# A fused attention and two-FFN kernel: the first token pair goes over to seven-product form two hidden blocks earlier, and the steps in front of it are laid out anew

## The chip, the cores and the metric

The kernel runs on one core of one Trainium2 chip. The metric is the device time of one execution in microseconds (us); the kernel before takes 1032.87 us (median of 3 runs, 1032.5 to 1033.78). The engines are called PE (TensorE), DVE (VectorE), ACT (ScalarE), POOL (GpSimd) and SP (SyncE, which issues loads).

## The reference

Everything is fp32. Tokens N = 6016, width C = 256, hidden width 2048.

```python
qn = q / (norm(q, axis=1) + 1e-6);  kn = k / (norm(k, axis=1) + 1e-6)
a  = softmax(kn.T @ qn / tau)                    # 256 x 256
x  = v @ a                                       # 6016 x 256
h  = x @ w_in;   x1 = (h * sigmoid(1.702 * h)) @ w_out
h2 = x1 @ w2_in; out = (max(h2, 0) + alpha * min(h2, 0)) @ w2_out
```

q, k, v and x arrive as fp32. The weights reach the device as 8-byte words (`raw`), which the kernel turns into fp32 with bit and multiply steps.

## The kernel before, in words

**Products in three passes.** Each fp32 operand is split into a high and a low part in fp32r; a product is three matmuls of 128 x 512 (`PASSES`: high x high, weight-high x token-low, weight-low x token-high), summed in PSUM (`product`, line 783).

**Tiling.** Tokens come in 12 chunks, two by two: a pair p holds chunks 2p and 2p+1. The hidden width is 16 tiles, taken two by two: j = 0..7. For one pair and one j, the first matrix (`WI`) gives four hidden blocks ("units"), each through an activation on ACT (`act`), a cast to its high part on ACT (`high`) and a subtraction on DVE (`low`, line 878). The second matrix (`WO`) then adds each unit into output accumulators in PSUM. Those 24 matmuls (`Outs.next`, called eight times) are laid between the products of the next j.

**Two ways to the four units.** `direct` (line 884) takes eight products. `quartet` (line 906) takes seven, in Strassen's manner, in the order A11, S1, A12, S2, S3, A22, S4. It needs sums of weight blocks (S1 to S4, made by `combine`: one whole-sum step, four small sums, a cast on ACT, a low word on DVE) and sums of token blocks (T1 to T4, made by `prepare`, each again with a subtraction, an ACT cast and a DVE low word). S2's result is copied out of its bank by ACT before S3's product adds to the same bank (`copy(a)`). In the first pair of layer 1 (l = 0), j < `STRASSEN` = 6 runs `direct`, the last two j run `quartet`; all later pairs run `quartet`.

**The first pair makes its own weights.** Attention is folded into the first matrix: W = E^T W1I is computed on PE while the first pair runs. For j >= 4 this goes by pairs of j (`emit_pair`, line 717): two halves m of six matmuls (`pw`), each kept by ACT (`activation`, the high part) and DVE (`scalar_tensor_tensor`, the low part). A "place" is one unit of `direct`: place 4j+i. `PAIRS` gives the place of pair 4 (j = 4, 5) as 13 and of pair 6 (j = 6, 7) as 21. The tiles that hold the converted W1I (`wi_hi`, `wi_lo`, line 339) have one buffer each: what is converted for pair 6 goes where pair 4's lay.

**Conversion.** A W1I or W1O piece goes through `scale` (ACT), `shift`, `power`, `rest` (DVE), `copy` (the high part, ACT), and then either `less` and `low` (two DVE steps) or, for pieces with `added`, a summing DMA from POOL (`sent`) and one DVE step (`split`). Three raw buffers hold loads; a load is asked for when an earlier piece's `rest` is done.

**What sets the order.** The program order on each engine is written by `beside(time)` (line 750): after each unit it pours DVE steps into a budget of microseconds, taking the step with the earliest `due` from the conversion and from the list `bg`. ACT's casts are put off into a list and emitted at the next `beside`. `need` and `finish` force what must be done. Each engine's instructions stand in the order in which they are written.

Of the kernel before, what the change touches and what calls it, by code (L numbers as in the profile page):

```python
# [30 lines left out]
FREE = ((0.7, 2.8, 1.7), (0.0, 0.8, 0.8))  # L31
FIRST = 2.1
AHEAD = 2
QK_PARTS = [1, 3] + [4] * 9 + [2, 2, 2, 1]
TAIL = 12
LOADING = 3
LANDING = 3
STRASSEN = 6
ON_VECTOR = (4, 5, 6, 8)
# [7 lines left out]
def f32(ap):  # L47
    return ap.bitcast(F32)
# [11 lines left out]
def attention_then_two_ffns(ctx: ExitStack, tc: tile.TileContext, q, k, vT, tau, w1i, w1o, w2i, w2o, alpha, outT):  # L60
# [129 lines left out]
    class Converter:  # L190


        STEPS = (("shift", 0.45), ("power", 0.45), ("rest", 0.63), ("less", 0.63), ("low", 0.63))
        ADDED = (("shift", 0.45), ("power", 0.45), ("rest", 0.63))

# [30 lines left out]
        def time(self, piece):  # L226
            if not piece or self.landed():
                return 0.63
            return self.list(piece)[self.at][1]
# [35 lines left out]
        def step(self):  # L265

            if self.waits():
                if not self.open:
                    self.scale(True)
                scalar_work()  # L270
            if not self.next() or self.landed():
                self.settle()
                return 0.63
# [35 lines left out]
        def due(self):  # L309
            return min(x.due for x in self.left())  # L310

        def place(self):
            self.now += 1
            if self.ahead and Convert.deep:
                self.scale()
                if self.flying and self.now - self.flying[0].begun >= LANDING:
                    self.ask()
# [13 lines left out]
    with tc.manual_schedule():  # L331
# [26 lines left out]
        def outer(j, n=1):  # L358
            def pair():
                return tuple(WO[:, j:j + n, h].rearrange("p q a b -> p q (a b)") if n > 1 else flat(WO[:, j, h]) for h in range(2))  # L360
            return Convert(w1o[:, j * PIECE:(j + n) * PIECE].rearrange("p (a n) -> p a n", a=1), pair, added=j > 3)

# [267 lines left out]
        def prepare(l, p):  # L630
# [20 lines left out]
            def minus(nm, a, b):  # L651
# [4 lines left out]
                ("B11", B11), ("B21", B21), ("T1", None), ("T2", None), ("T3", None), ("T4", None), ("B22", B22))}  # L656
            D = 0.63
            early = [
# [18 lines left out]
            if (l, p) == (0, 0):  # L677
                def last():
                    ops["T4"] = operand()
                    tmp["T4"] = tmp["T2"]  # L680
                    minus("T4", B21, "T2")
                steps = [early[i] for i in (2, 3, 6, 7)] + [late[0], Step(D, None, last, hi["T4"])] + [late[i] for i in (4, 5)]
                for x, due in zip(steps, (4, 4, 4, 4, 3, 3, 3, 3)):
                    x.due = LAST - due
                return steps
            return early, late

        def combine(hi, lo, hi_s, lo_s):
# [20 lines left out]

            steps = [Step(0.63, None, whole, kind=1), Step(0.9, None, sums_, high, 1), Step(0.63, high, low, kind=1)]  # L710
            combining.append(steps)
# [4 lines left out]

        def emit_pair(j):

            conv.need([ia[j], ia[j + 1]])
            for m in range(2):  # L720
# [28 lines left out]

        def beside(time, convert=False, place=None, most=None):  # L750
# [6 lines left out]
            while True:  # L757
                heads = [next((x for x in bg if x.kind == k), None) for k in (0, 1)]
                own = next((x for x in sorted(bg, key=lambda x: x.due) if x in heads and x.time <= time and not x.waits() and x.needs not in late), None)
                more = (conv.left() and conv.cost() <= time and not conv.waits()  # L760
                        and not any(x in late for x in conv.needs()))
                if own and not (more and (conv.due() <= own.due if Convert.deep else convert)):
                    time -= own.time
                    bg.remove(own)
                    own.run()
                elif more:
                    time -= conv.step()
                else:
                    if convert or place == 0:
                        spare[0] = min(time, 1.0)  # L770
                    return

# [111 lines left out]
        def direct(j, outs, mid_way):  # L884
# [3 lines left out]
            for i, (f, c) in enumerate((f, c) for f in range(2) for c in range(2)):  # L888
# [10 lines left out]
                u.high()  # L899
                mid_way(i)  # L900
                beside(FIRST, most=2 if (j, i) == (STRASSEN - 1, 3) else 3)
                u.low()
                units.append((f, c, u.pair))
            return Outs(0, 0, j, units)

        def quartet(l, p, j, outs, carry):
# [6 lines left out]
            def bank():  # L913
                return psh.tile([P, T], F32, tag="h", name="ps_h")
# [15 lines left out]
            fork = (l, p, j) != (1, 0, 0)  # L930
            a, b = bank(), bank()
            product(a, j, A11, ops["B11"], n, True, True)
# [20 lines left out]
            if j != 1:  # L953
                beside(FREE[l][0], place=0, most=most)
            if fork:
# [11 lines left out]
            if before:  # L967
                b12.low()
            outs.next()
            product(a, j, S2, ops["T2"], n, False, True)  # L970
            u2 = copy(a)
# [5 lines left out]
            outs.next()  # L977
            beside(FREE[l][1], most=most)
            finish(late[:4])
            product(a, j, S3, ops["T3"], n, False, True)  # L980
            u3 = copy(a)
# [3 lines left out]
            evacuate()  # L985
            beside(FREE[l][2], most=most)
            finish(late)
            u22.act()
            product(a, j, A22, ops["T4"], n, False, True)
# [14 lines left out]
            return Outs(l, p, j, [(0, c0, u11.pair), (1, c1, u22.pair), (1, c0, u21.pair), (0, c1, u12.pair)])  # L1004

        operands[0, 0] = blocks
        conv.ahead = True
# [27 lines left out]
        small = [flat(G), Convert.pool.tile([P, T], F32, tag="top", name="second", bufs=3)]  # L1035
        sums0, pair1 = [], []
        outs, carry = None, []
# [21 lines left out]
        def combining_of(n):  # L1059
            combined[n] = combine_wi(n)  # L1060
            for x in combined[n]:
                x.due = LAST + 3 * ((n or NQ) - STRASSEN) - 1
            bg.extend(combined[n])

        def mid_way(i):
            at = 4 * j + i
            if j < 3 and i == 1:
                if j == 0:
                    conv.need([ob_[0]])
                emit_w(j + 1)  # L1070
            for n, due in PAIRS.items():
                if at == due:
                    emit_pair(n)
                    for m in (n, n + 1):
                        if m >= STRASSEN:
                            combining_of(m)
            if j == 2 and i == 0:
                nc.sync.dma_start(alpha_sb, alpha)
            if at == LAST - 10:
                sums0.extend(prepare(0, 0))  # L1080
                bg.extend(sums0)
            if at == LAST - 2:
                combining_of(0)
            next_pair()

        for j in range(NQ):
# [5 lines left out]
            finish(combined[j])  # L1092
            finish(sums0)
            next_pair()
# [152 lines left out]
```

## Time and profile before

| | us |
|---|---|
| median of 3 runs | 1032.87 |
| profiled execution, its own time | 1033.06 |
| span of that execution | 1031.3 |
| PE busy | 1025.7 |
| DVE busy | 750.5 |
| ACT busy | 758.5 |

The span is the time from the first to the last instruction; 1.8 us lie around it. A busy PE is not proof that PE never waits, since the ends of matmuls are modelled and overlap; the starts of the matmuls show the pace: six of them take 1.36 us, 0.2267 us each.

### The profile page before, as it was taken

To read this page: it belongs to the slowest core of one execution; us is meant where nothing else is said; L and a number is where in the kernel's file an instruction comes from. 1 tells how busy PE (TensorE), PEld (TensorE's weight loads), DVE (VectorE), ACT (ScalarE), POOL (GpSimd) and SP (SyncE) were. 2 spreads that over 40 slices of the span, in tenths; PEclk is the share of its full clock that TensorE was granted. 3 is DMA by queue.
4 is the path that set the end of the run, shared out by engine and by line. 5 is a ranking of instruction groups with operands and counts; after the bars stand their busy time and mean duration, and the time that the engine had idled before them with its cause. 6 is when DMAs were issued, how large, how long until landed. Compare 5 with 4: busy or idle time off the path is not lost.

```text
span 1031.3 us, 12536 instructions
## 1 busy us (share of the span) xinstructions
PE 1025.7 (99%) x4634; PEld 865.4 (84%) x4634; DVE 750.5 (73%) x1226; ACT 758.5 (74%) x1273; POOL 38.4 (4%) x50
## 2 busy tenths in 40 slices
PE   9999999999999999999999999999999999999998
PEld 8888888888888888888998888888888888888997
DVE  4788888877778765445637877787877787877766
ACT  6787787778778766666767777777777777867776
POOL 4401000000000000000100000000000000000000
PEclk9999999999999999999999999999999999999999
DMA  9737222224325312003553001001001000000100
GB/s 356 266 106 178 65 74 70 98 80 168 114 89 179 113 41 77 1 1 132 196 168 113 1 21 62 1 21 62 1 21 62 1 18 25 36 0 1 41 1 36
DMA packets 32445, 79.72 MB, mean 77 GB/s; under 512 B 3200, under 2 KB 7808, under 8 KB 32384
## 3 DMA queue, kind: packets, MB, share of 16 engines
q1 hardware_dynamic: 28928, 65.29, 18.3%
q0 software_dynamic: 3456, 13.63, 4.6%
q8 instruction: 36, 0.59, 0.2%
q14 instruction: 25, 0.20, 0.1%
HBM read 52.96 MB, written 23.86 MB: 74 GB/s over the span
## 4 chain that ended last, share of the span: by engine, by line
PE 99%; DMA 0%; SPq 0%; ACT 0%; issue 0%
PE ps_o L814 50%; PE ps_h L785 44%; PE gram L433 4%; PE pw L567 1%; PE pw L723 1%; DMA qk<-in_k 0%; SPq L453 0%; PE nrm L510 0%; ACT s L831 0%; PE bc L532 0%; PE pt L555 0%
## 5 line engine op out<-in xcount | busy, mean ns | idle before, releaser
L814 PE MATMUL ps_o<-ghi,wo 128*128 128x512 f32 (+1 forms) x1536 | 561.0, 385 | 0.0
L785 PE MATMUL ps_h<-x,wi 128*128 128x512 f32 (+1 forms) x2034 | 548.1, 385 | 0.0
L785 PEld LDWEIGHTS ps_h<-x,wi 128*128 128x128 f32 x2034 | 381.2, 188 | 71.9 <-DVE wi L579 0.4
L814 PEld LDWEIGHTS ps_o<-ghi,wo 128*128 128x128 f32 x1536 | 288.4, 188 | 53.7
L814 PE MATMUL ps_o<-glo,wo 128*128 128x512 f32 (+1 forms) x768 | 296.1, 386 | 0.0
L851 DVE TENSOR_TENSOR g<-ps_h,s 128x512 f32<-128x512 f32 (+1 forms) x177 | 120.1, 679 | 103.9 <-PE ps_h L785 63.5
L880 DVE SCALAR_TENSOR_TENSOR glo<-g,sign_sb,ghi 128x512 fp32r<-128x512 f32 (+1 forms) x192 | 141.5, 737 | 55.4 <-ACT ghi L874 51.0
L923 ACT COPY s<-ps_h 128x512 f32<-128x512 f32 (+1 forms) x177 | 102.2, 577 | 106.4 <-PE ps_h L785 102.2
L882 DVE TENSOR_TENSOR glo<-g,ghi 128x512 fp32r<-128x512 f32 (+1 forms) x192 | 126.4, 677 | 65.9 <-ACT ghi L876 65.1
L814 PEld LDWEIGHTS ps_o<-glo,wo 128*128 128x128 f32 x768 | 144.2, 188 | 27.2 <-DVE glo L880 0.3
L874 ACT ACTIVATE ghi<-g,sign_sb 128x512 fp32r<-128x512 f32 (+1 forms) x192 | 137.2, 714 | 16.3 <-DVE g L870 10.9
L876 ACT CAST ghi<-g 128x512 fp32r<-128x512 f32 (+1 forms) x192 | 113.1, 612 | 3.4
L862 ACT ACTIVATE g<-ps_h 128x512 f32<-128x512 f32 (+1 forms) x108 | 63.3, 586 | 41.6 <-PE ps_h L785 41.1
L866 ACT ACTIVATE g<-g,sign_sb 128x512 f32<-128x512 f32 (+1 forms) x97 | 69.4, 716 | 29.2 <-DVE g L851 28.7
L870 DVE SCALAR_TENSOR_TENSOR g<-g,slope_sb 128x512 f32<-128x512 f32 (+1 forms) x97 | 71.6, 738 | 16.7 <-ACT g L866 16.6
L870 DVE SCALAR_TENSOR_TENSOR g<-ps_h,slope_sb,g 128x512 f32<-128x512 f32 (+1 forms) x95 | 69.7, 734 | 0.0
L934 ACT COPY ps_h<-ps_h 128x512 f32<-128x512 f32 (+1 forms) x89 | 50.2, 564 | 26.4 <-PE ps_h L785 26.1
L866 ACT ACTIVATE g<-ps_h,sign_sb 128x512 f32<-128x512 f32 (+1 forms) x95 | 64.3, 676 | 1.9 <-PE ps_h L785 0.2
L862 ACT ACTIVATE g<-g 128x512 f32<-128x512 f32 (+1 forms) x84 | 52.3, 622 | 13.8 <-DVE g L851 13.3
L433 PE MATMUL gram<-qk 128*128 128x256 f32 x156 | 34.3, 380 | 1.0 <-DMA qk<-in_k 1.0
L433 PEld LDWEIGHTS gram<-qk 128*128 128x128 f32 x156 | 29.4, 190 | 5.2 <-issue 1.4
L649 DVE TENSOR_TENSOR x<-t,x 128x512 fp32r<-128x512 f32 (+1 forms) x48 | 32.0, 674 | 0.0
(123 smaller groups left out, 493.5 us busy)
## 6 DMA issues: line engine op xcount, KB each, us to landing
wi<-w2i POOLq DMA_DIRECT2D x8, 896.0 KB, 4.9
xraw<-in_vT SPq DMA_DIRECT2D x10, 512.0 KB, 5.5
x<-ob SPq DMA_DIRECT2D x20, 256.0 KB, 2.9
xraw<-x SPq DMA_DIRECT2D x10, 512.0 KB, 3.7
out_T<-ob SPq DMA_DIRECT2D x20, 256.0 KB, 2.0
qk<-in_q SPq DMA_DIRECT2D x9, 512.0 KB, 10.3
qk<-in_k SPq DMA_DIRECT2D x9, 512.0 KB, 10.6
raw<-in_w1i SPq DMA_DIRECT2D x8, 512.0 KB, 5.0
```

Of the source, the lines that this page charges most:

```text
L433: nc.tensor.matmul(gram[m][:, :C], tiles[i][:, 1, r, m * P:(m + 1) * P], tiles[i][:, 0, r, :], start=(t == 0), stop=(t == R - 1))
L785: nc.tensor.matmul(ps[:, :n], WI[:, wq, a, blk], x[:, b, :n], start=(start and i == 0), stop=(stop and i == 2), skip_group_check=True)
L814: nc.tensor.matmul(acc_ps[c][d][:, :n], WO[:, j, a, f, d * P:(d + 1) * P], (hi, lo)[b][:, :n], start=(start and i == 0), stop=(stop and i ...
L851: nc.vector.tensor_tensor(self.src, ps[:, :self.n], s[:, :self.n], ALU.add)
L862: nc.scalar.activation(self.g, self.src, AF.Gelu_apprx_sigmoid)
L866: nc.scalar.activation(self.g, self.src, AF.Copy, scale=sign_sb[:, self.f])
L870: nc.vector.scalar_tensor_tensor(self.g, self.src, slope_sb[:, self.f], self.g, ALU.mult, ALU.max)
L874: nc.scalar.activation(self.hi, self.g, AF.Copy, scale=sign_sb[:, self.f])
L876: nc.scalar.copy(self.hi, self.g)
L880: nc.vector.scalar_tensor_tensor(self.lo, self.g, sign_sb[:, self.f], f32(self.hi), ALU.mult, ALU.subtract)
L882: nc.vector.tensor_tensor(self.lo, self.g, f32(self.hi), ALU.subtract)
L923: nc.scalar.copy(s[:, :n], ps[:, :n])
```

## The change

Four things are edited. **One:** `STRASSEN` goes from 6 to 4, so j = 4 to 7 of the first pair run `quartet`. **Two:** pair 6 is made at place 15 in place of 21, and `emit_pair` is called from inside `beside`: both halves' matmuls and ACT's high parts come first, and DVE's low parts follow with other DVE steps between. **Three:** the W1O pieces 2 and 3 are converted with the summing DMA as well; dues of the steps move; T1 to T4 of the first pair are each forced only in front of their own product (`operands_of`), where before all were forced in front of the quartet. **Four:** in layer 1, the first halves of the evictions of chunks 9, 10 and 11 are copied by DVE in place of ACT. The core of the diff:

```diff
-STRASSEN = 6
+MADE, BEFORE, BETWEEN = 1.2, 1.3, .65
+STRASSEN = 4
@@ outer
-            return Convert(..., added=j > 3)
+            return Convert(..., added=j >= 2)
-        PAIRS = {4: 13, 6: min(21, LAST - 2)}
+        PAIRS = {4: 13, 6: 15}
@@ prepare, (l, p) == (0, 0)
-                for x, due in zip(steps, (4, 4, 4, 4, 3, 3, 3, 3)):
-                    x.due = LAST - due
+                for x, due in zip(steps, (-1, 0, -1, 0, 1, 1, 1, 1)):
+                    x.due = LAST + due
@@ emit_pair
-        def emit_pair(j):
-            conv.need([ia[j], ia[j + 1]])
+        def emit_pair(j, steps):
+            halves = []
             for m in range(2):
                 ...
                 nc.scalar.activation(hi, src, AF.Copy, scale=rs[:, m:m + 1])
+                halves.append((lo, src, hi))
+            for m, (lo, src, hi) in enumerate(halves):
+                steps(m)
                 nc.vector.scalar_tensor_tensor(lo, src, rs[:, m:m + 1], f32(hi), ALU.mult, ALU.subtract)
@@ beside
+            for n in pairs:
+                time += MADE
+                def steps(m):
+                    nonlocal time
+                    first = min(time, (BEFORE, BETWEEN)[m])
+                    time += take(first) - first
+                emit_pair(n, steps)
+                for m in (n, n + 1):
+                    if m >= STRASSEN:
+                        combining_of(m)
+            time = take(time)
@@ evacuate
-                    copies = (nc.scalar.copy, nc.vector.tensor_copy)
+                    copies = (nc.vector.tensor_copy if not l and c > 8 else nc.scalar.copy, nc.vector.tensor_copy)
@@ direct
-                mid_way(i)
-                beside(FIRST, most=2 if (j, i) == (STRASSEN - 1, 3) else 3)
+                now = mid_way(i)
+                beside(FIRST + (0.5 if (j, i) in MORE else 0), most=2 if now or (j, i) == (STRASSEN - 1, 3) else 3, pairs=now)
+        def operands_of(which):
+            finish([x for i, x in enumerate(sums0) if (0, 1, 0, 1, 2, 3, 2, 3)[i] <= which])
@@ quartet: operands_of(0) before A11, (1) before S2, (2) before S3, (3) before A22
+            free = (0.9, 3.1, 2.1) if narrow and j < NQ - 1 else FREE[l]
@@ mid_way
-                    emit_pair(n)
+            for n in now:
+                conv.need([ia[n], ia[n + 1]])
@@ main loop
             finish(combined[j])
-            finish(sums0)
```

The lines of the changed file are shifted against the profile's by up to 34; `wi_hi`'s cast is line 151 before and 153 after, the keep of a half's high part 726 and 729.

**ACT around pair 4.** Before, where pair 6 is made, eight places after pair 4: `g` and `ghi` are a unit's activation and cast, `wi_hi<-p` a cast of converted W1I (here the one for pair 6), `wi<-pw` the keep of a half.

```order
L151 CAST wi_hi_1028<-p_872 128x2x256 [waits DMASW3_49]
L862 ACTIVATE g_1051<-ps_h_1036 128x512 [waits PE_49]
L876 CAST ghi_1049<-g_1051 128x512 [waits Activation_49]
L138 ACTIVATE p_1054<-raw_947 128x512 [waits DMAHW1_49,DVE_49]
L151 CAST wi_hi_1028<-p_918 128x2x256 [waits DMASW4_49]
L862 ACTIVATE g_1079<-ps_h_1064 128x512 [waits PE_49]
```

After, the same casts for pair 6 (`wi_hi_889`) stand here, at places 12 and 13, around the unit of place 13 (`g_914`) and pair 4's two keeps (`pw_918`, `pw_926`).

```order
L140 ACTIVATE p_887<-raw_808 128x512 [waits DMAHW7_49,DVE_49]
L153 CAST wi_hi_889<-p_755 128x2x256 [waits DMASW3_49,PE_49]
L883 ACTIVATE g_914<-ps_h_899 128x512
L897 CAST ghi_912<-g_914 128x512 [waits Activation_49]
L153 CAST wi_hi_889<-p_800 128x2x256 [waits DMASW4_49]
L729 ACTIVATE wi_436<-pw_918,rs_127 128x2x256
L729 ACTIVATE wi_436<-pw_926,rs_127 128x2x256
L883 ACTIVATE g_965<-ps_h_950 128x512 [waits PE_49]
```

Pair 6's first cast moved in front of pair 4's keeps; it waits for PE, and the activation and the two keeps behind it, which read PE's results, carry no wait for PE of their own.

**DVE in the first quartet.** Before, from A12 of the quartet j = 6 to its S3: `glo` is a unit's low part, `t`, `s` and `wi<-s` are `combine`'s steps, `t<-xraw` a step for the next pair's T1, `wo` a W1O piece, `g<-ps_h,second` the add that makes unit u22.

```order
L653 TENSOR_TENSOR t_1214<-xraw_1109,xraw_1107 128x512 [waits DMAHW3_49,DMAHW2_49]
L882 TENSOR_TENSOR glo_1202<-g_1203,ghi_1201 128x512 [waits PE_49,Activation_49]
L165 TENSOR_TENSOR wo_74<-p_1004,wo_74 128x512 [waits DMASW6_49,Activation_49]
L882 TENSOR_TENSOR glo_1218<-g_1247,ghi_1217 128x512 [waits PE_49,Activation_49]
L705 TENSOR_TENSOR wi_436<-s_1208,wi_436 128x512 [waits DVE_49]
L694 TENSOR_TENSOR t_1267<-wi_436 128x512
```

After, from T2's low word (`x_1013`) to T4's (`x_1082`) in the quartet j = 4; `x_1079` is T3's.

```order
L652 TENSOR_TENSOR x_1013<-t_1014,x_1013 128x512 [waits Activation_49]
L903 TENSOR_TENSOR glo_1025<-g_1059,ghi_1024 128x512 [waits Activation_49]
L656 TENSOR_TENSOR t_1080<-xraw_377 128x512
L656 TENSOR_TENSOR t_1014<-xraw_375,t_1014 128x512 [waits DVE_49]
L708 TENSOR_TENSOR wi_436<-s_1054,wi_436 128x512 [waits Activation_49]
L167 TENSOR_TENSOR wo_74<-p_858,wo_74 128x512 [waits DMASW6_49]
L157 TENSOR_SCALAR p_970<-top_1021 128x512
L652 TENSOR_TENSOR x_1079<-t_1080,x_1079 128x512 [waits Activation_49]
L872 TENSOR_TENSOR g_1093<-ps_h_1041,second_533 128x512 [waits Activation_49]
L652 TENSOR_TENSOR x_1082<-t_1014,x_1082 128x512 [waits Activation_49]
```

T2's, T3's and T4's low words moved from the places before the quartet into it, each behind other DVE steps.

**ACT in the same quartet, after:** from the fork copy out of A11's bank to T4's cast. `G` and `second` take S2's and S3's results out of their bank.

```order
L964 COPY ps_h_1033<-ps_h_1032 128x512 [waits PE_49]
L648 CAST x_1013<-t_1014 128x512 [waits DVE_49]
L140 ACTIVATE p_1052<-raw_895 128x512 [waits DMAHW1_49]
L883 ACTIVATE g_1059<-ps_h_1033 128x512 [waits PE_49]
L897 CAST ghi_1024<-g_1059 128x512 [waits Activation_49]
L947 COPY G_123<-ps_h_1032 128x512 [waits PE_49]
L153 CAST wo_74<-p_858 128x512 [waits DMASW6_49]
L711 CAST wi_436<-s_1054 128x512 [waits DVE_49]
L648 CAST x_1079<-t_1080 128x512 [waits DVE_49]
L947 COPY second_533<-ps_h_1032 128x512 [waits PE_49]
L648 CAST x_1082<-t_1014 128x512 [waits DVE_49]
```

The cast of `combine` (`wi<-s_1054`) that DVE's low word waits for stands two places behind the copy of S2's result.

## Rows read from the trace of the kernel before

**Rows 1.** The page, part 1: engine, busy us, share, instructions.

```profile
PE 1025.7 (99%) x4634; PEld 865.4 (84%) x4634; DVE 750.5 (73%) x1226; ACT 758.5 (74%) x1273; POOL 38.4 (4%) x50
```

**Rows 2.** The waits of PE, all of them: us, times, longest.

```profile
PE idle L391 <- POOL ones L384: 1.1, 1, 1.1
PE gram L433 <- DMA qk<-in_k: 1.0, 1, 1.0
```

**Rows 3.** Windows: us, busy by engine, granted clock, DMA share, GB/s.

```profile
6.00:8.00 2.00, 1.00 (x5) 0.68 (x4) 0.00 (x0) 0.77 (x1) 0.00 (x0) 1.00 1.02 378
...
80.00:100.00 20.00, 20.00 (x89) 16.54 (x89) 15.75 (x29) 14.42 (x26) 2.60 (x3) 1.00 0.72 177
```

**Rows 4.** Timeline of PE: pair 4, places 14 and 16: start, us, instruction.

```profile
88.21 0.62 PE L723 MATMUL pw<-wi_hi,eT_hi 128*128 128x512 f32 x2
...
90.94 0.85 PE L785 MATMUL ps_h<-x,wi 128*128 128x512 f32 x3
...
96.38 0.84 PE L785 MATMUL ps_h<-x,wi 128*128 128x512 f32 x3
```

**Rows 5.** The chain that ended last, in order of time: two quartets.

```profile
156.40 1.36 PE ps_o L814 x6
...
166.60 1.36 PE ps_o L814 x6
```

**Rows 6.** Timeline of PE and ACT: the unit of place 5.

```profile
62.14 0.85 PE L785 MATMUL ps_h<-x,wi 128*128 128x512 f32 x3
...
65.34 0.62 ACT L151 CAST wi_hi<-top 128x512 fp32r<-128x512 f32 x1 [1.12 <-DVE top L142]
...
66.44 0.59 ACT L862 ACTIVATE g<-ps_h 128x512 f32<-128x512 f32 x1
```

**Rows 7.** Timeline of ACT: a keep, a scaling and casts, a copy.

```profile
91.14 0.69 ACT L726 ACTIVATE wi<-pw,rs 128x512 fp32r<-128x512 f32 x1 [0.68 <-PE pw L723]
91.72 0.65 ACT L138 ACTIVATE p<-raw 128x512 f32<-128x512 f32 x1
...
98.10 0.65 ACT L138 ACTIVATE p<-raw 128x512 f32<-128x512 f32 x1
98.66 0.58 ACT L862 ACTIVATE g<-ps_h 128x512 f32<-128x512 f32 x1
99.27 0.62 ACT L876 CAST ghi<-g 128x512 fp32r<-128x512 f32 x1
99.80 0.62 ACT L151 CAST wo<-p 128x512 fp32r<-128x512 f32 x1
...
125.84 0.59 ACT L920 COPY G<-ps_h 128x512 f32<-128x512 f32 x1
126.33 0.62 ACT L645 CAST x<-t 128x512 fp32r<-128x512 f32 x1
```

**Rows 8.** Timeline of DVE: keeps, conversion steps, a unit's low part, weight sums.

```profile
91.86 0.75 DVE L727 SCALAR_TENSOR_TENSOR wi<-pw,rs,wi 128x512 fp32r<-128x512 f32 x1 [0.62 <-ACT wi L726]
92.53 0.68 DVE L158 SCALAR_TENSOR_TENSOR p<-raw,p 128x512 f32<-128x512 uint32 x1
93.13 0.42 DVE L142 TENSOR_SCALAR top<-p 128x512 uint32<-128x512 uint32 x1
93.58 0.43 DVE L155 TENSOR_SCALAR p<-top 128x512 uint32<-128x512 uint32 x1
93.93 0.69 DVE L882 TENSOR_TENSOR glo<-g,ghi 128x512 fp32r<-128x512 f32 x1
...
116.36 0.75 DVE L727 SCALAR_TENSOR_TENSOR wi<-pw,rs,wi 128x512 fp32r<-128x512 f32 x1 [0.62 <-ACT wi L726]
117.15 0.69 DVE L694 TENSOR_TENSOR t<-wi 128x512 f32<-128x512 f32 x1
117.87 0.29 DVE L699 TENSOR_TENSOR s<-t 128x128 f32<-128x128 f32 x1
...
118.61 0.28 DVE L702 TENSOR_TENSOR s<-t,s 128x128 f32<-128x128 f32 x1
```

**Rows 9.** Line 133, the loads of raw weights: us from issue to landing.

```profile
DMA to landing us min/median/max: 3.5/4.0/9.0
```

More of the change, by code (lines that the diff above doesn't have):

```diff
@@ L32 @@
 FIRST = 2.1
+MORE = (0, 1), (1, 1), (2, 1)
 AHEAD = 2
@@ L190, in attention_then_two_ffns @@
     class Converter:
-        STEPS = (("shift", 0.45), ("power", 0.45), ("rest", 0.63), ("less", 0.63), ("low", 0.63))
-        ADDED = (("shift", 0.45), ("power", 0.45), ("rest", 0.63))
+        STEPS = (("shift", 0.45), ("power", 0.45), ("rest", 0.62), ("less", 0.62), ("low", 0.62))
+        ADDED = (("shift", 0.45), ("power", 0.45), ("rest", 0.62))
         def __init__(self):
@@ L227, in time @@
             if not piece or self.landed():
-                return 0.63
+                return 0.62
             return self.list(piece)[self.at][1]
@@ L272, in step @@
                 self.settle()
-                return 0.63
+                return 0.62
             if not self.open:
@@ L309, in due @@
         def due(self):
-            return min(x.due for x in self.left())
+            return min(x.due - (0 if x in self.flying else 4 if x.added else 1) for x in self.left())
         def place(self):
@@ L315, in place @@
                 self.scale()
-                if self.flying and self.now - self.flying[0].begun >= LANDING:
+                x = self.flying[0] if self.flying else None
+                if x and self.now - x.begun >= LANDING + (self.now < 4 * STRASSEN and x.due - self.now > 1):
                     self.ask()
@@ L360, in pair @@
                 return tuple(WO[:, j:j + n, h].rearrange("p q a b -> p q (a b)") if n > 1 else flat(WO[:, j, h]) for h in range(2))
-            return Convert(w1o[:, j * PIECE:(j + n) * PIECE].rearrange("p (a n) -> p a n", a=1), pair, added=j > 3)
+            return Convert(w1o[:, j * PIECE:(j + n) * PIECE].rearrange("p (a n) -> p a n", a=1), pair, added=j >= 2)
         ia, ob_ = {}, {}
@@ L656, in prepare @@
                 ("B11", B11), ("B21", B21), ("T1", None), ("T2", None), ("T3", None), ("T4", None), ("B22", B22))}
-            D = 0.63
+            D = 0.62
             early = [
@@ L708, in high @@
                 nc.scalar.copy(hi_s(), box["s"])
-            steps = [Step(0.63, None, whole, kind=1), Step(0.9, None, sums_, high, 1), Step(0.63, high, low, kind=1)]
+            steps = [Step(0.62, None, whole, kind=1), Step(0.9, None, sums_, high, 1), Step(0.62, high, low, kind=1)]
             combining.append(steps)
@@ L748, in first, with beside @@
             bg[k:k] = steps
-        def beside(time, convert=False, place=None, most=None):
+        def beside(time, convert=False, place=None, most=None, pairs=()):
             conv.place()
@@ L756, in beside, with take @@
             spare[0] = 0.0
[L757 to L771, printed above, removed]
+            def take(time):
+                while True:
+                    heads = [next((x for x in bg if x.kind == k), None) for k in (0, 1)]
+                    own = next((x for x in sorted(bg, key=lambda x: x.due) if x in heads and x.time <= time and not x.waits() and x.needs not in late), None)
+                    more = (conv.left() and conv.cost() <= time and not conv.waits()
+                            and not any(x in late for x in conv.needs()))
+                    if own and not (more and (conv.due() <= own.due if Convert.deep else convert)):
+                        time -= own.time
+                        bg.remove(own)
+                        own.run()
+                    elif more:
+                        time -= conv.step()
+                    else:
+                        return time
+            for n in pairs:
[9 more added lines that the diff above has]
+            time = take(time)
+            if convert or place == 0:
+                spare[0] = min(time, 1.0)
         def finish(steps):
@@ L928, in quartet @@
             most = 1 if l else 2 if narrow else None
+            free = (0.9, 3.1, 2.1) if narrow and j < NQ - 1 else FREE[l]
             u11, u22, u21, u12 = (Unit(l, 2 * j + f, c) for f, c in ((0, c0), (1, c1), (1, c0), (0, c1)))
             fork = (l, p, j) != (1, 0, 0)
+            if narrow:
+                operands_of(0)
             a, b = bank(), bank()
@@ L953, in quartet @@
             if j != 1:
-                beside(FREE[l][0], place=0, most=most)
+                beside(free[0], place=0, most=most)
             if fork:
@@ L969, in quartet @@
             outs.next()
+            if narrow:
+                operands_of(1)
             product(a, j, S2, ops["T2"], n, False, True)
@@ L977, in quartet @@
             outs.next()
-            beside(FREE[l][1], most=most)
+            beside(free[1], most=most)
             finish(late[:4])
+            if narrow:
+                operands_of(2)
             product(a, j, S3, ops["T3"], n, False, True)
@@ L985, in quartet @@
             evacuate()
-            beside(FREE[l][2], most=most)
+            beside(free[2], most=most)
             finish(late)
+            if narrow:
+                operands_of(3)
             u22.act()
@@ L1004, in quartet @@
             return Outs(l, p, j, [(0, c0, u11.pair), (1, c1, u22.pair), (1, c0, u21.pair), (0, c1, u12.pair)])
+        sums0 = []
         operands[0, 0] = blocks
@@ L1061, in combining_of @@
             for x in combined[n]:
-                x.due = LAST + 3 * ((n or NQ) - STRASSEN) - 1
+                x.due = LAST + 3 * ((n or NQ) - STRASSEN) - 2
             bg.extend(combined[n])
@@ L1070, in mid_way @@
                 emit_w(j + 1)
-            for n, due in PAIRS.items():
-                if at == due:
-                    emit_pair(n)
-                    for m in (n, n + 1):
-                        if m >= STRASSEN:
-                            combining_of(m)
+                if j + 1 >= STRASSEN:
+                    combining_of(j + 1)
+            now = [n for n, due in PAIRS.items() if at == due]
+            for n in now:
+                conv.need([ia[n], ia[n + 1]])
             if j == 2 and i == 0:
                 nc.sync.dma_start(alpha_sb, alpha)
-            if at == LAST - 10:
+            if at == 7:
                 sums0.extend(prepare(0, 0))
                 bg.extend(sums0)
-            if at == LAST - 2:
-                combining_of(0)
             next_pair()
+            return now
         for j in range(NQ):
```

4 lines of the change are left out of this document (3 added, 1 removed).

## The prediction, made before the changed kernel ran

> **What bounds the kernel now.** I read the page's busy part first: PE is busy 99% of the span, DVE and ACT under three quarters [rows 1]. Then PE's waits: two, both in the first 8 us, 2.1 us together [rows 2]. So between the first load and the end PE waits for nobody for more than its modelled ends hide, and the time is the number of matmuls times their pace. The chain of waits gives the pace: six matmuls take 1.36 us, 0.2267 each, and the same place of two successive quartets lies 166.60 - 156.40 = 10.20 us apart, 45 matmuls at that pace [rows 5]. The granted clock is 1.00, the 2.4 GHz level [rows 3]. Last I read the stretch that the change rebuilds, unit by unit: the first pair from place 13 on [rows 4, 7, 8]. There DVE is busy 15.75 us of 20 [rows 3], so it has some air, but PE has none: whatever makes it wait is added to the time in full, and cannot be caught up later.
>
> **What is removed.** A direct j takes 24 + 24 matmuls, a quartet 21 + 24. Two j's go over: 6 matmuls, 6 x 0.2267 = -1.36 us. That is the whole of what PE can gain: pair 6 still needs its 12 matmuls, at place 15.
>
> **What the rebuilt front adds: one wait on ACT.** Pair 4's matmuls start at 88.21 and end at 90.94, where the next product starts [rows 4]. In the changed order ACT casts pair 6's first high part ahead of place 13's activation and of pair 4's two keeps. The buffer of that cast is the one that pair 4's twelve matmuls read. The order shows that the wait is for the last of them: the keeps, which need these matmuls' results, stand behind it without a wait of their own. So ACT stands until 90.94 + 0.20 (the second keep started at 91.14 in the same situation [rows 7]). That a waiting ACT instruction holds back ready ones is in the trace: place 5's product ends at about 62.14 + 0.68, but its activation starts at 66.44, behind a cast that waited 1.12 us for DVE [rows 6].
>
> ACT from there, start to start by [rows 7] (after a cast 0.53, after an activation 0.61, after a keep 0.58): cast 91.14, activation 91.67, cast 92.28, second cast for pair 6 92.81, keeps 93.34 and 93.92, activation 94.50, cast 95.11, T1's cast 95.64; then it waits for the weight sums.
>
> DVE waits for the first of these casts with pair 6's first low part (91.14 + 0.62, and 0.04 to start: 91.80), though by the same steps it is free some 3 us before. Behind it, by [rows 8]: five plain steps of 0.60 and a power of 0.45, to 95.25; a keep (0.67), a shift (0.35), a keep (0.79), the whole sum (0.72) and the four small sums (0.74 to the last, which takes 0.28). End: 91.80 + 3.45 + 2.53 + 0.74 + 0.28 = 98.80. ACT casts the sum at 98.84, and then a scaling (99.37), an activation (99.93), a cast (100.54) and the high part of W1O's piece 3 at 101.07, done at 101.69.
>
> PE, from 96.38 [rows 4]: pair 6 to 99.11, A11's product to 99.79, then the first output matmul, which reads that piece 3. It is to be had at 101.73. **Stall 1.94.** Its third pass needs the piece's low part: DVE has the sums' low word at 99.50, power 100.10, rest 100.55, a unit's low 101.15, that low part 101.75, done 102.44, where PE is due at 102.18: **0.30**. S1's product takes a bank that DVE's keep for pair 6 reads until 103.70 (T2's subtraction 102.35, the keep 102.95); due 102.71: **1.03**. Its second pass needs T1's low word, 103.62 to 104.31; due 103.97: **0.38**. So 3.65 us are gone by S1.
>
> **What the quartet adds.** T2, T3 and T4 are no longer ready when their products come, and their low words stand behind steps that wait.
> - T2: behind T1's low word come a keep, a whole sum, a shift, a unit's low and four sums (0.60 + 0.67 + 0.60 + 0.35 + 0.60 + 0.74 + 0.20 = 3.76 after 103.62): T2's low word at 107.38, done 108.07. S2's second pass would be at 103.42 + 3.65 = 107.07. **1.04**.
> - T3: its low word stands behind the weight sums' low word, which waits for a cast on ACT that stands behind the copy of S2's result. Count from S2's last matmul, 108.56: copy 108.76 (0.20), another cast 109.25 (0.49), the cast 109.78, done 110.40; DVE 110.44, 111.04, 111.64, T3's low word 111.99, done 112.68: 4.16 us after S2. PE has six output matmuls and one pass to fill that, 1.59 us. **2.57**, and this does not hang on how late DVE was before.
> - T4: its low word stands behind the add that makes u22, which needs the copy of S3's result: from S3's end 0.20 + 0.59 + 0.04 for the add, 0.60, and 0.69 + 0.04 for T4, 2.16 in all, against the same 1.59. **0.57**.
>
> Sum of stalls: 3.65 + 1.04 + 2.57 + 0.57 = 7.83. The later quartets have T1 to T4 made, and their weight sums stand a quartet ahead; I take nothing there.
>
> **What I cost at nothing.** Two more summing DMAs replace two DVE steps (1.2 us less on DVE, hidden by PE). Two quartets' weight sums come into the first pair and leave the second, which lightens DVE there, behind PE either way. Three evictions go from ACT to DVE at the end of layer 1: one plain step of about 0.6 us each, behind the next quartet's products; were that cover gone, 1.8 us together.
>
> **Two bounds.** The wait on the shared buffer does not occur in the run before, so its price stands between two ends: nothing, if what is behind it has time to spare, and all of the stalls down to S1's and the lateness of T2, 3.65 + 1.04. I take the upper, since the DVE chain of 7 us behind the wait has no idle time in it. The load of pair 6's first raw piece is asked for only some three places ahead of its scaling; loads landed after 3.5 to 9.0 us, 4.0 in the median [rows 9]. I take the median, which leaves pair 4's own low part about 1.4 us of time.
>
> **Sum.** 7.83 - 1.36 = +6.47. On the profiled execution, 1033.06, that is 1039.5; the median of the runs is 0.19 lower, so 1039.3.
>
> **Clock.** In the stretch from 6 to 8 us PE is busy for half the time and the granted clock stays 1.00 [rows 3]. "TensorE: Matmul & The Clock Gate" of the Trainium skill (section "Why this matters for your kernels") warns of idle gaps between bursts of matmuls, after which the array goes on at half clock. By that rule the stalls would cost a second time; no run here shows a fall, and by the row it costs nothing. Worked out as a rival below.
>
> **The rivals.**
> - *Only the quartet's own order costs.* The buffer's wait is harmless, and DVE is in time for T1. Then T2 waits only for pair 6's second keep (ACT 99.31 to 100.00, DVE 100.04, then the same 3.16 us of steps and 0.69: 103.89; due 103.42, 0.51 with the start), T3 2.57, T4 0.57: 3.65 - 1.36 = +2.29, 1035.2. For it: ACT and DVE have idle time in this stretch before. Against: the keeps without a wait of their own.
> - *Not slower: everything is hidden.* PE loses only its six matmuls: 1031.5, which is no change by measurement. The place is S3 of the first quartet and the price -1.36; it decides itself at 1.59 us after S2's end, by which T3's low word would have to be done. For it: in every later quartet PE waits for no one [rows 2]. Against: the order has T3's low word behind a step that hangs on S2's copy.
> - *The clock falls.* After the first stall PE goes on at 1.2 GHz for up to a quartet: 45 more times 0.2267 = 10.2 at most, 1040 to 1049.
> - *The load lands late.* At 9.0 us pair 4's low part comes about 2.6 us after PE wants it, and all that follows moves along: 1042.
>
> **Chances.** My sum 0.68, the quartet alone 0.16, all hidden 0.08, the clock 0.03, the late load 0.05. A measurement of this kernel tells about 0.2% (2.1 us) from no change. Faster than that would need more than the 1.36 us that PE can lose: 0.02, within it 0.10 (all hidden, and the lower part of the quartet alone), slower 0.88. The range takes in most of the quartet alone and the late load, and leaves out the hidden case, the fallen clock and the edges: 1034.8 to 1042.
>
> **What would show it.** In the changed profile, an ACT cast of `wi_hi` that waits about 2 us or more for PE's `pw`, and DVE idle for some 3 us ahead of pair 6's low part; PE idle in `ps_o` for ACT's `wo` by about 2 us near 100, in `ps_h` for DVE's `wi` and `x` near 103 to 108, and the longest at S3 for T3's low word; no new wait of PE after the first quartet, quartets 10.20 us apart, and six matmuls fewer. I am wrong if PE's waits sum to less than 4 us, if ACT's cast does not wait for PE, or if PE waits in other quartets.

## The result, and the profile after

The changed kernel takes 1041.87 us (median of 5 runs, 1040.60 to 1042.37) against 1032.90 for the kernel before in the same comparison: a ratio of 1.0085, 95% interval 1.0074 to 1.0097. It is slower by 9.0 us. 1039.3 us had been predicted, range 1034.8 to 1042.0. The profiled execution is the shortest of the five, 1040.60 us with a span of 1038.8.

Page, part 1, and all waits of PE after the change (us in total, times, longest), against [rows 1, 2]:

```profile
PE 1028.6 (99%) x4628; PEld 865.2 (83%) x4628; DVE 752.9 (72%) x1231; ACT 759.7 (73%) x1276; POOL 40.1 (4%) x52
...
PE ps_h L806 <- DVE x L652: 2.0, 2, 1.2
PE ps_o L835 <- ACT wo L153: 1.8, 1, 1.8
PE idle L394 <- POOL ones L387: 1.1, 1, 1.1
PE ps_h L806 <- ACT x L648: 0.9, 1, 0.9
PE ps_h L806 <- DVE wi L733: 0.8, 1, 0.8
```

Six matmuls fewer, and five new waits (in four lines), all in the first quartet; the wait of 1.0 us for `qk` in the first 8 us is gone. The wait list shows only what is left beyond the modelled ends; what PE really loses is read from starts. Timeline of PE after, from pair 6's end on (start, us, instruction, and in brackets the idle time and its releaser), against [rows 4]:

```profile
98.40 0.85 PE L806 MATMUL ps_h<-x,wi 128*128 128x512 f32 x3
101.02 0.50 PE L835 MATMUL ps_o<-ghi,wo 128*128 128x512 f32 x1 [1.77 <-ACT wo L153]
101.35 0.40 PE L835 MATMUL ps_o<-glo,wo 128*128 128x512 f32 x1
101.78 0.50 PE L835 MATMUL ps_o<-ghi,wo 128*128 128x512 f32 x1
103.05 1.32 PE L806 MATMUL ps_h<-x,wi 128*128 128x512 f32 x3 [0.76 <-DVE wi L733]
104.21 0.39 PE L835 MATMUL ps_o<-ghi,wo 128*128 128x512 f32 x1
...
106.25 0.39 PE L806 MATMUL ps_h<-x,wi 128*128 128x512 f32 x1
107.38 0.73 PE L806 MATMUL ps_h<-x,wi 128*128 128x512 f32 x2 [0.74 <-DVE x L652]
...
109.10 0.39 PE L835 MATMUL ps_o<-ghi,wo 128*128 128x512 f32 x1
110.34 0.50 PE L806 MATMUL ps_h<-x,wi 128*128 128x512 f32 x1 [0.85 <-ACT x L648]
112.09 1.22 PE L806 MATMUL ps_h<-x,wi 128*128 128x512 f32 x2 [1.25 <-DVE x L652]
113.11 0.63 PE L835 MATMUL ps_o<-ghi,wo 128*128 128x512 f32 x1
113.54 0.63 PE L835 MATMUL ps_o<-glo,wo 128*128 128x512 f32 x1
```

Three matmuls from 98.40 at 0.2267 each end the issue at 99.08; the next starts at 101.02: 1.94 lost. In this way each start, less the one before it and its matmuls' pace, gives the table below. From 112.09 to 114.82 the matmuls are 0.43 to 0.5 us apart, about half pace. The granted clock says why (windows of after: us, busy by engine, granted clock, DMA share, GB/s):

```profile
105.00:110.00 5.00, 3.75 (x16) 2.44 (x14) 4.29 (x11) 3.07 (x6) 0.00 (x0) 1.00 0.12 12
110.00:115.00 5.00, 3.41 (x8) 2.52 (x9) 3.07 (x6) 1.94 (x5) 0.00 (x0) 0.67 0.54 198
115.00:120.00 5.00, 5.00 (x24) 4.11 (x23) 3.74 (x8) 3.73 (x7) 0.00 (x0) 0.99 0.00 0
```

A clock of 0.67 over 5 us and 0.99 over the next 5 is some 3.4 us at half clock (0.33 x 5 x 2, and 0.01 x 5 x 2).

ACT and DVE after, where the prediction put the start of it all, against [rows 7, 8]:

```profile
90.42 0.62 ACT L153 CAST wi_hi<-p 128x512 fp32r<-128x512 f32 x1 [2.35 <-PE pw L726]
...
91.08 0.69 DVE L167 TENSOR_TENSOR wi_lo<-p,wi_hi 128x512 fp32r<-128x512 f32 x1 [2.47 <-ACT wi_hi L153]
```

ACT's cast for pair 6 waits 2.35 us for pair 4's matmuls, and DVE behind it 2.47.

In later quartets PE loses a little twice, near 127 and 290. In the quartet j = 5, S4's product starts 0.41 us behind the matmul before it, since its bank is still read by u22's sum (DVE's add, 126.45 to 127.13):

```profile
126.78 0.39 PE L835 MATMUL ps_o<-ghi,wo 128*128 128x512 f32 x1
127.19 1.67 PE L806 MATMUL ps_h<-x,wi 128*128 128x512 f32 x6
```

A second execution of the changed kernel was profiled later (below). What PE lost, us:

| place | predicted | first profile | second profile |
|---|---|---|---|
| W1O piece 3, high and low part | 1.94 + 0.30 | 2.24 | 2.23 |
| bank held by pair 6's keep, at S1 | 1.03 | 1.04 | 1.04 |
| T1's low word | 0.38 | 0.48 | 0.48 |
| T2 | 1.04 | 1.02 | 0.99 |
| T3 | 2.57 | 2.53 | 2.65 |
| T4 | 0.57 | hidden by the half clock | 0.66 |
| half clock | 0 | 1.50 | 0 |
| pair 4's low part | 0 | 0 | 0.32 |
| u22's sum in later quartets (near 127 and 290) | 0 | 0.65 | 0.62 |
| sum | 7.83 | 9.46 | 8.99 |

Less 1.36 for six matmuls that is +8.10 for the first execution and +7.63 for the second. In both, pair 4 starts earlier than in the profile before (87.50 and 87.67 instead of 88.21: less waiting in the first 8 us), so +7.39 and +7.09. Measured against that profile, 1033.06, are +7.54 and +7.30: 0.15 and 0.21 stay unaccounted for. (Against the execution of before that ran beside the second, 1032.76, it is +7.60; that one has no profile, so its first 8 us are not known.) Executions differ by some 0.7 us in when the first `pw` matmul starts (48.03 to 48.79 over all profiles), and an account against a median closes no better than that.

### The profile page after: what moved, and what is told of

Its sections match the earlier page's. It is cut to its first block, busy times and chain, and to the rows that moved or that the text cites. A ratio compares the mean times of both kernels' runs of the same rounds, so it can differ in the third digit from the quotient of the medians.

```text
span 1038.8 us, 12543 instructions
## 1 busy us (share of the span) xinstructions
PE 1028.6 (99%) x4628; PEld 865.2 (83%) x4628; DVE 752.9 (72%) x1231; ACT 759.7 (73%) x1276; POOL 40.1 (4%) x52
## 4 chain that ended last, share of the span: by engine, by line
PE 93%; DVE 1%; ACT 0%; issue 0%
PE ps_o L835 49%; PE ps_h L806 43%; PE pw L570 1%; PE pw L726 0%; DVE wi L733 0%; DVE glo L903 0%; DVE x L652 0%; DVE t L697 0%; DVE wo L167 0%; DVE t L656 0%; DVE p L157 0%; ACT wi L711 0%; DVE wi L708 0%; DVE wi_lo L167 0%; DVE top L144 0%
## 5 line engine op out<-in xcount | busy, mean ns | idle before, releaser
L883 ACT ACTIVATE g<-ps_h 128x512 f32<-128x512 f32 (+1 forms) x104 | 60.8, 585 | 32.1 <-PE ps_h L806 31.0
L883 ACT ACTIVATE g<-g 128x512 f32<-128x512 f32 (+1 forms) x88 | 54.9, 623 | 15.8 <-DVE g L872 15.3
```

The lines of the kernel that those rows point to most:

```text
L883: nc.scalar.activation(self.g, self.src, AF.Gelu_apprx_sigmoid)
```

## The experiments

Theory 1 is the prediction's: the wait on the shared `wi_hi` buffer is the price of everything down to T2. Theory 2: DVE has more to do there than time, with or without that wait. Theory C: the granted clock falls behind the stalls and costs a part of the time. Times of before beside the runs: 1032.58 (own buffers, own buffers without sums, the 14 matmuls, five direct j), 1032.76 (the changed kernel again), 1032.70 (the other four).

**Own buffers for pair 6.**

```diff
-t = wi_whole[j] = wi_first.pop() if wi_first else wi_tiles()
+t = wi_whole[j] = (wi_first.pop() if wi_first else wi_tiles() if j < 6
+    else [xin[1].tile([P, 2, T], F32R, tag=f"x{i}", ...) for i, h in ((8, "hi"), (9, "lo"))])
```

> The changed kernel, and pair 6's high and low words of W1I get buffers of their own (two operand slots that lie unused until the second pair), so that ACT's cast for pair 6 no longer waits for pair 4's matmuls. The order of the instructions on ACT and DVE stays as it is. Theory 1 (the prediction's price: the shared buffer's wait makes all the stalls of PE down to S1 and the lateness of T2, 3.65 + 1.04 us): the wait goes, PE's waits fall to about 3.1 us, the time to about 1036. Theory 2 (DVE has more work in this stretch than time, and would be late without the wait): only the W1O stall of about 1.9 us in ps_o goes, the stalls at S1, T2, T3 and T4 stay, and the time is about 1039 to 1040. In both DVE no longer waits 2.5 us for a wi_hi cast near 91.

1038.87 us, ratio 1.0060 (1.0047 to 1.0073). ACT and DVE at the same two instructions, and PE's waits:

```profile
89.00 0.61 ACT L153 CAST wi_hi<-p 128x512 fp32r<-128x512 f32 x1
...
89.64 0.69 DVE L167 TENSOR_TENSOR wi_lo<-p,wi_hi 128x512 fp32r<-128x512 f32 x1 [0.36 <-ACT wi_hi L153]
```

```profile
PE ps_h L806 <- DVE x L652: 2.0, 2, 1.3
PE idle L394 <- POOL ones L387: 1.1, 1, 1.1
PE ps_h L806 <- ACT x L648: 0.8, 1, 0.8
PE ps_h L806 <- DVE wi L733: 0.8, 1, 0.8
PE ps_o L835 <- ACT wo L153: 0.3, 1, 0.3
```

ACT's cast has no wait any more, and the low word on DVE comes 1.44 us earlier (91.08 in the changed kernel). Only the W1O stall shrank, from 2.24 to 0.76 by the starts; S1 1.03, T1 0.48, T2 1.00 and T3 2.64 stay as they were. Theory 1 falls: the wait was priced at 4.69 and is worth about 1.5 by the starts. By the medians it is 2.7 (1041.87 - 1032.90 less 1038.87 - 1032.58); at a mean clock of 1.0 the executions lie 1.6 to 2.3 apart (1040.36 against 1038.02 and 1038.74), so a part of the 2.7 is likely the clock. From 89.64 to 107.7 DVE's rows follow one another without an idle entry: it is late without the wait. ACT, on which the W1O piece's cast stands, is not the late engine; it idles there for DVE's sums:

```profile
96.67 0.62 ACT L711 CAST wi<-s 128x512 fp32r<-128x512 f32 x1 [2.45 <-DVE s L705]
```

**Own buffers, and no weight sums for j = 4 and 5.** `combine`'s DVE and ACT instructions for these two j are not issued, while their place in the plan stays.

> As the run with own buffers, and the weight sums for j = 4 and j = 5 are left out (their seven DVE steps and one ACT cast each; the products with S1 to S4 read other blocks of the same weights instead, so that PE's work is the same in number and shape). Theory 2 (DVE's load): with some 4.5 us less on DVE between pair 6 and S3, the stalls at S1, T1 and T2 go, and those at T3 and T4 (about 2.9 us, since these steps stand behind a copy of the quartet itself) stay: about 1034.5 to 1036, near 4 us less than with own buffers alone. Theory 1: these stalls were the buffer's, so leaving the sums out changes little against own buffers alone (under 1 us).

1036.06 us, ratio 1.0033 (1.0021 to 1.0045): 2.8 us less than with own buffers alone, where near 4 were expected (PE's loss by the starts is 3.7 less). PE, at S3:

```profile
105.94 0.49 PE L809 MATMUL ps_h<-x,wi 128*128 128x512 f32 x1 [0.60 <-ACT x L648]
107.43 0.85 PE L809 MATMUL ps_h<-x,wi 128*128 128x512 f32 x2 [1.00 <-DVE x L652]
108.08 0.63 PE L839 MATMUL ps_o<-ghi,wo 128*128 128x512 f32 x1
108.50 0.63 PE L839 MATMUL ps_o<-glo,wo 128*128 128x512 f32 x1
```

No loss is left from 88 to 105: with the sums' steps go W1O, S1, T1 and T2. Theory 2 holds. T3 stays, 0.76 + 1.26 = 2.02 against 1.01 + 1.52 = 2.53 in the changed kernel, though the sums' cast and low word, behind which the prediction put T3's low word, are not issued here. Its subtraction on DVE stands directly behind a unit's low part, which waits for ACT's cast in the same quartet:

```profile
103.94 0.69 DVE L907 TENSOR_TENSOR glo<-g,ghi 128x512 fp32r<-128x512 f32 x1 [1.63 <-ACT ghi L901]
104.55 0.69 DVE L656 TENSOR_TENSOR t<-xraw 128x512 f32<-128x512 f32 x1
```

So most of T3's stall seems to come from where its steps stand in the quartet, not from the one wait that was named; the next run moves them. The clock falls again behind it (0.43 us from matmul to matmul between 108.08 and 111.06, 1.71 lost with the start behind the stall).

**The same, and T2's to T4's steps all issued ahead of S2.** The sums are left out as before.

```diff
             if narrow:
-                operands_of(1)
+                operands_of(3)
             product(a, j, S2, ops["T2"], n, False, True)
```

> As the run with own buffers and without the weight sums of j = 4 and j = 5 (these sums are left out), and all steps of T2, T3 and T4 that are still open are issued ahead of S2's product instead of ahead of S2, S3 and A22 one by one. Theory 2 (three causes that add up: the shared buffer's wait, DVE's load, and the place of T3's and T4's steps behind the copies of S2's and S3's results): the last 2.8 us of stalls at S3 and A22 go too, PE waits for less than 1 us in the first pair, the granted clock stays 1.00, and the time is at or just under before's, 1032.0 to 1032.9. Theory 1 (T3's and T4's lateness comes from before the quartet): they stay late, about 1035 to 1036.

1033.54 us, ratio 1.0008 (0.9999 to 1.0017). The waits of PE, all of them:

```profile
PE idle L394 <- POOL ones L387: 1.1, 1, 1.1
```

T4's stall is gone and T3's is down to 0.43, so they came from the place of these steps in the quartet. By the starts 0.58 is left in pair 4 besides, and three times 0.3 to 0.4 behind u22's sum: 2.0 in all, less 1.36, +0.65 against +0.84 by the medians. The expected 1032.0 to 1032.9 missed these.

**Matmuls into the stalls at T2 and T3** (14 that nobody reads, at the changed kernel), and **into T2's, T3's and T4's with own buffers** (16). The core of the first edit; the second has two such matmuls at A22 as well.

```diff
+def fill(ps, k):
+    for _ in range(k):
+        nc.tensor.matmul(ps, WI[:, 4, 0, 0], blocks[0, 0][:, 0], start=True, stop=True, ...)
...
-product(a, j, S2, ops["T2"], n, False, True)
+product(a, j, S2, ops["T2"], n, False, True, gap=(b, 4) if narrow and j == STRASSEN else None)
+if narrow and j == STRASSEN:
+    fill(b, 4)
-product(a, j, S3, ops["T3"], n, False, True)
+product(a, j, S3, ops["T3"], n, False, True, gap=(b, 6) if narrow and j == STRASSEN else None)
```

> The changed kernel, and while PE waits for T2's low word and for T3's two words in the first quartet it does 14 matmuls that nobody reads (4 ahead of S2's second pass, 4 ahead of S3's first, 6 ahead of its second; 0.2267 us each, 0.91 + 0.91 + 1.36 us, each less than the wait that it fills: 1.2, 1.1 and 1.7 us), into a bank that is free by then. Nothing else changes. Theory C (the granted clock falls after the stalls and costs a part of the time): the clock stays at 1.00 from 105 to 125 us, the half-speed matmuls near 113 us go, and the time is 1 to 2 us shorter, 1040 to 1040.5. Rival (the clock costs nothing that the stall at T4 would not have cost): the same time as the changed kernel, 1041.9; and if the fillers make PE later than its operands, longer.

1041.59 us (four executions, 1040.61 to 1042.72), ratio 1.0087 (1.0074 to 1.0101): the time of the changed kernel. In the profiled execution, the shortest, the clock is 1.00 where it had been 0.67, but the other three have mean clocks of 0.997 to 0.998. So filling these stalls did not keep the clock up, or did not in every execution; the first two stalls, 2.24 and 1.04, had stayed. By time this is a miss for theory C. Nor does the profile show that the filling helped: the second profile of the changed kernel (below) has a clock of 1.00 there without it.

> As the run with own buffers, and while PE waits for T2's, T3's and T4's words in the first quartet it does 16 matmuls that nobody reads (4 ahead of S2's second pass, 4 and 6 ahead of S3's first and second, 2 ahead of A22's second). With own buffers the stall of 1.8 us at the W1O piece is gone as well, so that of all stalls only S1's (about 1.1 us) stays open. Theory C (the clock falls after the stalls, and that made own_buffers 1 us slower than its stalls alone): the clock is 1.00 in every execution, and the time is 1037.3 to 1038.0, against 1038.9 with own buffers. Rival (the clock costs nothing): 1038.9, unchanged.

1038.28 us (1038.07 to 1038.57), ratio 1.0054 (1.0041 to 1.0066), against 1038.02 to 1039.30 with own buffers alone. The mean clock is 0.999 or 1.0 in each of the five, against 0.998 in three of the five. The stretch at S3, first of this run, then with own buffers alone:

```profile
110.00:115.00 5.00, 5.00 (x22) 3.55 (x22) 2.97 (x5) 3.11 (x6) 0.00 (x0) 1.00 0.29 111
```

```profile
110.00:115.00 5.00, 4.35 (x12) 3.42 (x13) 3.09 (x5) 2.31 (x5) 0.00 (x0) 0.68 0.31 120
```

The fillers (16 x 0.2267 = 3.63) and what is still lost (3.25) less 1.36 make +5.52; +5.58 was measured by the medians. Here, with most of the W1O stall gone too, the account needs no clock term. The 0.6 us less than with own buffers alone are under the 0.9 to 1.6 that were expected, and the two intervals overlap. The executions with own buffers alone say the same: 1038.02 and 1038.74 at a mean clock of 1.0, 1038.87 to 1039.30 at 0.998. So some 0.6 us is what the fallen clock cost beside the stalls, as an estimate.

**Five direct j.**

```diff
-STRASSEN = 4
+STRASSEN = 5
-        PAIRS = {4: 13, 6: 15}
+        PAIRS = {4: 13, 6: 17}
```

> The changed kernel with five direct j instead of four: STRASSEN 5, pair 6 at place 17 instead of 15. Three matmuls fewer than before instead of six (-0.68 us). The prediction's claim that T3's and T4's stalls (2.57 + 0.57 us) lie in the quartet's own order and do not hang on how late DVE was: 1032.9 - 0.68 + 3.14 = 1035.4. Theory 2 (the crowding of DVE): with a direct j more ahead of the first quartet, T1 to T4 are ready, PE waits for nobody, 1032.2 to 1032.7, no change that can be measured against before. Granted clock 1.00 throughout in both.

1033.01 us, ratio 1.0003 (0.9995 to 1.0012). The prediction's claim that T3's and T4's stalls do not hang on how late DVE was falls: with one direct j more, T3's and T4's low words run from 111.14 to 112.43, well ahead of S3's product at 115.93. What remains is u22's sum, 0.31 and 0.42, which eats the 0.68, so that the time is above the 1032.2 to 1032.7 that were expected.

**A version without these waits** (five direct j, pair 6 at place 18, T3's and T4's due times two places earlier, smaller budgets ahead of S3 and A22). The diff is against the run with five direct j.

```diff
-        PAIRS = {4: 13, 6: 17}
+        PAIRS = {4: 13, 6: 18}
-(-1, 0, -1, 0, 1, 1, 1, 1)
+(-1, 0, -1, 0, -1, -1, -1, -1)
-free = (0.9, 3.1, 2.1) if narrow and j < NQ - 1 else FREE[l]
+free = (0.9, 2.5, 1.5) if narrow and j < NQ - 1 else FREE[l]
```

> A version meant to beat both kernels: the changed kernel with five direct j, pair 6 at place 18, the due times of T3's and T4's steps two places earlier (-1 instead of 1), and 2.5 and 1.5 us instead of 3.1 and 2.1 us offered to the background steps ahead of S3 and A22. Followed by hand through its order, PE waits for nobody in the first pair: three matmuls fewer than before, -0.68 us, 1031.9 to 1032.3; against five_direct, in which PE lost 0.4 to 0.8 us behind u22's sum, 0.4 to 1 us less. Rival: what is left out of the count (the evictions, the later quartets) eats the 0.68 us, and it is the same as before.

1032.29 us (1031.95 to 1032.48), ratio 0.9996 (0.9987 to 1.0004). PE waits up to the first `pw` matmuls only (the second line is at 48.4 us):

```profile
PE idle L394 <- POOL ones L387: 1.1, 1, 1.1
PE pw L570 <- ACT eT_hi L563: 0.2, 1, 0.2
```

It beats the changed kernel by some 9 us; against before, 0.41 us less by the medians, the interval takes in no change. The two summing DMAs and the DVE evictions of the change are in it, so neither costs anything that shows; the summing DMAs by themselves were not run.

**The evictions alone, in the kernel before.**

```diff
-copies = (nc.scalar.copy, nc.vector.tensor_copy)
+copies = (nc.vector.tensor_copy if not l and c > 8 else nc.scalar.copy, nc.vector.tensor_copy)
```

> The kernel before, with the change's edit of the evictions alone: three of layer 1's last evictions go from ACT to DVE. The prediction costs it at nothing: the same as before, within 0.1%. Rival: the new DVE steps of about 0.6 us hold up a unit in the last quartet of layer 1, and PE waits up to 1.8 us: 1033 to 1034.5.

1032.74 us, ratio 1.0000 (0.9991 to 1.0009): nothing, as predicted.

**The changed kernel again.**

> The changed kernel once more, for a second profile. Its first profile is that of the shortest of its five executions (1040.60 us, mean clock 0.998; the other four 1041.44 to 1042.37 at 0.996 to 0.997). Theory C: a longer execution shows the same stalls of PE, within 0.3 us, and a longer stretch at a fallen clock between 100 and 125 us, which makes the difference. Rival (what differs from execution to execution lies elsewhere, as in the loads of the first 10 us): the stretch from 100 to 125 us looks as in the first profile, and the first quartets come later by as much as PE waited more in the first 10 us.

1040.36 us (one execution) at a mean clock of 1.0, so not the longer execution that was wanted. It shows the other case: the same stalls in the same places, and no fall of the clock. First the stretch, then PE at T4:

```profile
110.00:115.00 5.00, 2.92 (x10) 1.79 (x10) 3.26 (x6) 2.43 (x6) 0.00 (x0) 1.00 0.62 210
```

```profile
114.54 0.46 PE L806 MATMUL ps_h<-x,wi 128*128 128x512 f32 x1
115.31 0.73 PE L806 MATMUL ps_h<-x,wi 128*128 128x512 f32 x2 [0.31 <-DVE x L652]
```

At full pace T4's stall appears (0.54, and 0.12 behind it). In the first profile the slow matmuls lay over it, and its 1.50 also holds the 0.12 behind T3, so there the half clock cost 1.50 - 0.66 - 0.12 = 0.72 net.

Pair 4's matmuls lose 0.32 here:

```profile
87.67 0.66 PE L726 MATMUL pw<-wi_hi,eT_hi 128*128 128x512 f32 x2
88.33 0.73 PE L726 MATMUL pw<-wi_lo,eT_hi 128*128 128x512 f32 x2
```

ACT's scaling at 86.35 had waited 0.48 us for a load, and pair 4's last low part, behind it, ends at 88.27. ACT's cast for pair 6 then waits 1.65 us and DVE 1.77 instead of 2.35 and 2.47, and the stalls behind are the same: it is the end of the wait that sets them, not its length.

## Why the prediction was right, and where it was not

- **Direction, places and the releaser at each place: right.** ACT's wait is 2.35 us in the first profile and 1.65 in the second where "about 2 us or more" was named, DVE's 2.47 and 1.77 where "some 3 us"; the PE stalls came at the named places with the named releasers.
- **The range: held by luck.** The median, 1041.87, lies 0.13 us inside an edge that was drawn for the late load and meant to leave out the fallen clock. It is 2.6 us above the forecast, and the likely reason is the fallen clock (below). That edge is mis-added besides: a load at 9.0 us instead of 4.0, with 1.4 us of time, is 3.6 us late and not 2.6.
- **The sum of the stalls it names: right**, 7.83 against 8.05 in the execution at full clock; no term is off by more than 0.1. What it put at nothing adds 0.94 there. Following the printed order instruction by instruction with durations of the same forms was enough.
- **The price of the shared buffer: wrong.** "I take the upper, since the DVE chain of 7 us behind the wait has no idle time in it." The chain is late by itself. A wait shifts a chain once, here by 1.44 us on DVE; the prediction charged it with all lateness behind it. The rival "only the quartet's own order" had the mirror fault: it took DVE to be "in time for T1" without that wait, and did not follow the order for it; with own buffers the kernel is at 1038.87, not at 1035.2. The forecast did not suffer, since the sum was of what is lost, whoever causes it.
- **"This does not hang on how late DVE was before": wrong** in general. It is true for this order (T3 keeps 2.02 of 2.53 when the sums go), but the order itself comes from DVE's crowding. And the wait named for T3, the sums' cast behind S2's copy, is not what most of it hangs on: the stall stays without that cast.
- **"The later quartets ... I take nothing there": wrong by 0.6 us**, twice u22's sum, some 0.3 each with its restart. By the starts one of the prediction's own signs of being wrong came true ("if PE waits in other quartets"), though the wait list does not show it.
- **Pair 4's low part, taken to have "about 1.4 us of time": wrong in one of two profiles**, 0.32 lost behind a load that was waited for.
- **"Clock. ... by the row it costs nothing": wrong**, and given a chance of 0.03 as a rival. A row with one gap in the first 8 us said nothing on several gaps in 15 us. The first profile shows 0.67 and a net 0.72 us. "TensorE: Matmul & The Clock Gate" of the Trainium skill (section "Why this matters for your kernels") warns of idle gaps between bursts of matmuls, gaps longer than any single one here (the longest loss is 1.94 us). Three profiles show half clock behind these shorter gaps (0.67, 0.68 and 0.79 in a window of 5 us: the first profile, own buffers, own buffers without sums), and the second profile shows none. So the measurement goes beyond what the page warns of, and "By that rule the stalls would cost a second time" read the page more widely than it is written.

The 1041.87 is 1.3 to 1.5 us more than both profiled executions. The four longer ones have mean clocks of 0.996 to 0.997 against 0.998 and 1.0; the first profile's 0.998 is some 3.4 us at half clock (111.7 to 115.1). In other kernels of this case too the executions at a lower mean clock are the longer ones (own buffers, above; without the sums 1035.43 at 1.0, and 1035.95 to 1036.52 at 0.998). So a longer stretch at half clock is the likely cause, but none of the longer executions of the changed kernel was profiled: it was argued, not shown.

## What to carry to other kernels

When an engine is 99% busy, sum the lateness of each operand against it by following the printed order; here each named term held to a tenth of a microsecond. To say which edit causes it, follow the order a second time without the suspected wait: a wait is worth only the shift that it gives the chain, not the lateness that the chain has anyway. And where several stalls lie close together, put in a term for the clock.

## What the runs showed of the hardware that had not been expected

- The clock fell behind losses of 0.76 and 1.26 us (own buffers without sums, half pace from 108.08) and did not fall in one of two profiles of the changed kernel with 8.05 us of losses in the first quartet. What decides it stays open.
- PE's first matmuls after a stall come some 0.1 us further apart: 101.02 to 101.35 is 0.33, not 0.23. The 0.12 behind each of T2, T3 and T4 more than makes up the difference between 7.83 and 8.05.
